# The activation of a fused recurrence and MLP rewritten: tanh(e·U(log(1 + c·e))) with one polynomial in place of two

## The chip, the core and the metric

The kernel runs on one core of one Trainium2 chip. Its engines each have an instruction queue of their own that is worked through in order: TensorE (PE, whose weight loads appear as PEld), VectorE (DVE), ScalarE (ACT), GpSimd (POOL) and SyncE (SP), which issues the DMAs here. The metric is the device time of one execution in microseconds (us); lower is better.

## The reference: what is computed

The first half is a gated recurrence over 768 steps for 4 batches of 8 heads of size 48. Its output, laid out as 3072 tokens of 384 numbers, goes through an MLP with 2048 hidden units whose activation is h·erf(softplus(h)). All of it is float32; the two weights of the MLP arrive in float64 and are rounded on the chip.

```python
f = 1.0 / (1.0 + np.exp(-f_logit))
for t in range(S):
    state = f[:, :, t, :, None] * state + np.einsum('bhd,bhe->bhde', k[:, :, t], v[:, :, t])
    y[:, :, t] = np.einsum('bhd,bhde->bhe', q[:, :, t], state)
x = y.transpose(0, 2, 1, 3).reshape(B * S, H * D)
h = x @ w_in
sp = np.maximum(h, 0.0) + np.log1p(np.exp(-np.abs(h)))
out = (h * erf(sp)) @ w_out
```

## The kernel before

**First part.** The tokens are taken in 24 chunks of 128, all heads at once (`chunk`). A chunk brings f, q and k in by transposes on PE (L318), turns f into a sigmoid F on DVE and ACT (maximum L330, Exp L333 on ACT, add L334, reciprocal L335), copies q and k out of PSUM on ACT (L338), and then climbs seven levels. At each level PE multiplies k and q into scores (L352), DVE multiplies half of q by the decays of the neighbouring half (Q, L385; the first time L375), POOL does the same to k (K, L389) and folds the decays (T, L394), and the scores are kept through a mask by DVE (At, L363), at the two last levels by copies on ACT (L371). At the end PE forms the outputs y (L403, L407), which ACT copies (xs, L411), and a new state (L419 to L438); the outputs are transposed back (L443) and copied into xT (L445).

**Second part.** Three chunks make a block of 384 tokens; there are eight blocks. For a block, `second_part` forms the 16 tiles of hidden units on PE (hps, L275, three products each), ACT copies each out of PSUM (Hg, L283, with two PSUM buffers), and after every fourth tile `activation` works on the group of four, 128 x 1536 numbers, in place. A block has four groups, called g0 to g3 here. Then three output tiles are summed on PE over all 16 tiles of hidden units (ops, L289), copied by ACT (L298) and stored.

**The activation before.** ACT takes the magnitude (Abs, L255) and Exp (L256); four quadratics follow for log1p, each a Square with a bias column on ACT (L247) and one DVE instruction that adds a constant and multiplies it into z (L250). POOL clamps h (L258), DVE adds it (L261), ACT squares the sum (L262), three more quadratics follow for erf (L247 and L250), then Tanh on ACT (L264) and the product with h on DVE (L265). The tiles e, z and x have two buffers each, so at most two groups are under way.

**What sets the order.** The second part of one block is a generator from which `chunk` draws a number of matmuls at each level of the next block's chunks: the hidden tiles during the first two chunks, the output tiles during the third. From that order and the buffers a scheduler fixes one order for each engine's queue before the program runs. An instruction that waits holds up all that stands behind it on its engine. The first block's chunks run beside the rounding of the weights, and the last block's second part runs alone at the end.

Of the kernel before, what the change touches and what calls it, by code (L numbers as in the profile page):

```python
"""HGRN2 recurrence, then x @ w_in -> h * erf(softplus(h)) -> @ w_out, all in float32.

The recurrence runs in chunks of 128 tokens.  Within a chunk, a pair (s, t), s < t, is served at the
level h = 1, 2, .., 64 at which s and t lie in neighbouring halves of a block of 2h tokens:

    prod(f[s+1..t]) = prod(f[s+1 .. end of s's half]) * prod(f[start of t's half .. t])

so q and k only ever get multiplied by products of f, which are at most 1: nothing is divided by a
decay, and nothing can overflow, whatever f is.  Going one level up multiplies half of q and half of
k by the total of the neighbouring half.  After the last level q holds the decay since the chunk's  # L10
start and k the decay to its end, which is what the state between chunks needs.

softplus(h) = max(h, 0) + log1p(exp(-|h|)), and erf on [0, inf) is tanh(z * P(z * z)).  log1p(e) / e
and P are minimax polynomials (relative error 3.0e-8 of log1p and 9.6e-8 of erf, below one float32
ulp), taken as products of quadratics (k * x + a)**2 + b.

Weights given in float64 come as their bits and are rounded to float32 here.
"""
# [17 lines left out]
# log1p(e) = e * prod((k * e + a)**2 + b) on [0, 1]  # L36
LOG1P_K = 0.518609681
LOG1P_AB = (
    (0.523462696, 0.297482162),
    (-0.0426566012, 0.876115907),  # L40
    (-0.738881803, 0.726747093),
    (-1.20404919, 0.116298437),
)
# erf(z) = tanh(z * prod((k * z * z + a)**2 + b)) for z >= 0
ERF_K = 0.072173846
ERF_AB = (
    (0.453293936, 0.100843822),
    (-0.384392197, 1.24745854),
    (-1.51376175, 0.348741268),
)  # L50
# erf(z) is 1 in float32 from here on
Z_MAX = 6.0
# exp(-x) stays finite from here on
LOGIT_MIN = -87.0

P = 128
NBUF = 3  # chunks of q, k and f on chip
LOOK = 2  # chunks that the loads run ahead
# [5 lines left out]
def kernel(  # L64
# [13 lines left out]
    wpe = 1  # 32-bit words of a weight  # L78
# [3 lines left out]
    HP = H // 2  # pairs of heads: one at partitions 0.., one at 64..  # L82
    DP = 64  # a head's rows, padded
    NCH = S // P
    CPB = 3  # chunks in a block of tokens of the second part
# [4 lines left out]
    FG = 4  # tiles of d_ff that the activation takes at once  # L90
# [11 lines left out]
    def fixed(name, shape, dtype=FP32):  # L102
        return const.tile(shape, dtype, name=name)
# [7 lines left out]
    # masks[0] is the diagonal; masks[1 + n] the pairs of level 2**n, below a block's size  # L111
# [3 lines left out]
    erf_bias = fixed("erf_bias", [P, len(ERF_AB)])  # L115
    log_bias = fixed("log_bias", [P, len(LOG1P_AB)])

# [30 lines left out]
    def load_piece(i):  # L148
        """The DMA of a piece; one in float64 lands as its words, to be rounded."""
        dst, src = pieces[i]  # L150
        if wpe == 1:
            nc.sync.dma_start(out=dst, in_=src)
            return None
        raw = gpool.tile([P, wpe * PIECE], U32, name="raw", tag="Hg")
        nc.sync.dma_start(out=raw[:].rearrange("p (k f) -> p k f", k=dst.shape[1]), in_=src)
        return raw

    def round_piece(i, raw):
        """float64 to the nearest float32: sign, exponent and 20 bits of the high word are one
        float32, the low word is what comes to it, and what is below float32's range is 0."""  # L160
# [48 lines left out]
    for i, (a, _) in enumerate(ERF_AB):  # L209
        nc.vector.memset(erf_bias[:, i : i + 1], a)  # L210
    for i, (a, _) in enumerate(LOG1P_AB):
        nc.vector.memset(log_bias[:, i : i + 1], a)
# [9 lines left out]
    for n in range(n_masks - 1):  # L222
        # s ^ t has its highest bit at n, and it is t that has it
        same = fixed(f"same{n}", [P, P], I32)
        nc.vector.tensor_scalar(
            out=bit[:], in0=col[:], scalar1=n, scalar2=1,
            op0=ALU.logical_shift_right, op1=ALU.bitwise_and,
        )
        nc.vector.tensor_scalar(
            out=same[:], in0=row[:], scalar1=n, scalar2=None, op0=ALU.logical_shift_right  # L230
        )
        nc.vector.tensor_scalar(
            out=same[:], in0=same[:], scalar1=1.0, scalar2=None, op0=ALU.is_equal
        )
        nc.vector.tensor_tensor(out=masks[:, 1 + n, :], in0=same[:], in1=bit[:], op=ALU.mult)

# [1 line left out]
    def activation(Hg):  # L238
        n = FG * TB
        h = Hg[:].rearrange("p j t -> p (j t)")  # L240
        e = work.tile([P, n], FP32, name="e", tag="e")
        z = work.tile([P, n], FP32, name="z", tag="z")
        x = work.tile([P, n], FP32, name="x", tag="x")

        def times_quads(acc, first, arg, tmp, scale, ab, bias):
            for i, (_, b_) in enumerate(ab):
                nc.scalar.activation(  # L247
                    out=tmp[:], in_=arg[:], func=AF.Square, bias=bias[:, i : i + 1], scale=scale
                )
                nc.vector.scalar_tensor_tensor(  # L250
                    out=acc[:], in0=tmp[:], scalar=b_, in1=first[:] if i == 0 else acc[:],
                    op0=ALU.add, op1=ALU.mult,
                )

        nc.scalar.activation(out=e[:], in_=h, func=AF.Abs)  # L255
        nc.scalar.activation(out=e[:], in_=e[:], func=AF.Exp, scale=-1.0)  # L256
        times_quads(z, e, e, x, LOG1P_K, LOG1P_AB, log_bias)
        nc.gpsimd.tensor_scalar(  # L258
            out=x[:], in0=h, scalar1=Z_MAX, scalar2=0.0, op0=ALU.min, op1=ALU.max
        )  # L260
        nc.vector.tensor_tensor(out=z[:], in0=z[:], in1=x[:], op=ALU.add)  # L261
        nc.scalar.activation(out=e[:], in_=z[:], func=AF.Square)  # L262
        times_quads(z, z, e, x, ERF_K, ERF_AB, erf_bias)
        nc.scalar.activation(out=z[:], in_=z[:], func=AF.Tanh)  # L264
        nc.vector.tensor_tensor(out=h, in0=h, in1=z[:], op=ALU.mult)  # L265
# [55 lines left out]
    def chunk(g, xT, fill):  # L321
# [21 lines left out]
        def scores(h):  # L343
            """k^T q of the pairs of level h (0: the diagonal) and others, to PSUM as [s, t]."""
# [104 lines left out]
    n_slots = 1 + len(levels)  # times that a chunk pumps  # L449
# [43 lines left out]
```

## Time and profile before

| | us |
|---|---|
| median of 3 runs (1463.07, 1463.49, 1740.36) | 1463.49 |
| the profiled execution, its span from first to last instruction | 1460.2 |
| difference between that median and the span | 3.3 |
| period of a block in the steady part, profile | about 160 |

In the rows below, an instruction is named by engine, line and operation, then the tile it writes and those it reads, the shape, and how many there were. "Idle before" is time in which the engine stood still just ahead of such instructions, with the engine and line whose end released it.

### The profile page before, as it was taken

To read this page: it belongs to the slowest core of one execution; us is meant where nothing else is said; L and a number is where in the kernel's file an instruction comes from. 1 tells how busy PE (TensorE), PEld (TensorE's weight loads), DVE (VectorE), ACT (ScalarE), POOL (GpSimd) and SP (SyncE) were. 2 spreads that over 40 slices of the span, in tenths; PEclk is the share of its full clock that TensorE was granted. 3 is DMA by queue.
4 is the path that set the end of the run, shared out by engine and by line. 5 is a ranking of instruction groups with operands and counts; after the bars stand their busy time and mean duration, and the time that the engine had idled before them with its cause. 6 is when DMAs were issued, how large, how long until landed. Compare 5 with 4: busy or idle time off the path is not lost.

```text
span 1460.2 us, 15916 instructions
## 1 busy us (share of the span) xinstructions
PE 1111.4 (76%) x6456; PEld 738.6 (51%) x6456; DVE 985.4 (67%) x883; ACT 686.4 (47%) x693; POOL 430.6 (29%) x401
## 2 busy tenths in 40 slices
PE   3334697689968898789959897689957998789546
PEld 2234565356535565456536565456535665455323
DVE  8896357963797357963798367963797357970682
ACT  0000047731775147731775146731775146732872
POOL 2644224232243224231252224232243124330110
PEclk9999998769966788668976898769967798669868
DMA  9330011011101011011101011011101000000000
GB/s 248 119 87 6 17 23 22 0 22 39 23 0 22 17 22 22 1 22 38 23 0 22 17 23 22 1 26 35 23 0 22 17 1 1 1 6 11 0 0 16
DMA packets 108744, 37.19 MB, mean 25 GB/s; under 512 B 100480, under 2 KB 103552, under 8 KB 108672
## 3 DMA queue, kind: packets, MB, share of 16 engines
q1 hardware_dynamic: 108672, 36.18, 11.0%
q8 instruction: 51, 0.84, 0.2%
q14 instruction: 21, 0.17, 0.0%
HBM read 31.46 MB, written 4.72 MB: 25 GB/s over the span
## 4 chain that ended last, share of the span: by engine, by line
PE 42%; DVE 30%; POOL 13%; ACT 7%; issue 6%; SPq 1%; DMA 0%; POOLq 0%; DVEq 0%; ACTq 0%
DVE z L250 13%; PE ops L289 12%; PE sc L352 8%; PE hps L275 7%; POOL K L389 6%; PE y L403 5%; PE y L407 5%; DVE F L335 4%; DVE At L363 4%; POOL x L258 3%; POOL T L394 3%; ACT x L247 3%; DVE z L261 3%; DVE Q L385 2%; PE ps_t L318 1%
## 5 line engine op out<-in xcount | busy, mean ns | idle before, releaser
L289 PE MATMUL ops<-w_out_sb,Hg 128*128 128x384 f32 x768 | 338.3, 597 | 107.9 <-DVE Hg L265 107.9
L352 PE MATMUL sc<-Q,K 48*128 48x128 f32 (+2 forms) x3456 | 246.3, 297 | 196.1 <-POOL K L389 90.3
L250 DVE SCALAR_TENSOR_TENSOR z<-x,z 128x1536 f32<-128x1536 f32 x192 | 343.6, 1807 | 47.5 <-ACT x L247 46.9
L352 PEld LDWEIGHTS sc<-Q,K 48*128 48x128 f32 (+2 forms) x3456 | 208.3, 199 | 295.4 <-POOL K L389 139.9
L389 POOL TENSOR_TENSOR K<-K,T 128x256 f32<-128x256 f32 x144 | 194.6, 1352 | 411.9 <-PE sc L352 411.3
L275 PE MATMUL hps<-xT,w_in_sb 128*128 128x384 f32 x768 | 289.8, 516 | 11.7 <-ACT Hg L283 11.0
L289 PEld LDWEIGHTS ops<-w_out_sb,Hg 128*128 128x128 f32 x768 | 171.5, 234 | 232.6 <-DVE Hg L265 91.7
L247 ACT ACTIVATE x<-e,log_bias 128x1536 f32<-128x1536 f32 x128 | 201.1, 1572 | 32.2 <-DVE z L250 29.4
L275 PEld LDWEIGHTS hps<-xT,w_in_sb 128*128 128x128 f32 x768 | 142.8, 199 | 100.2 <-ACT Hg L283 18.7
L363 DVE COPY_PREDICATED At<-masks,sc 128x1024 f32<-128x1024 uint8 x144 | 186.6, 1296 | 0.0
L247 ACT ACTIVATE x<-e,erf_bias 128x1536 f32<-128x1536 f32 x96 | 151.3, 1576 | 61.5 <-DVE z L250 58.7
L385 DVE TENSOR_TENSOR Q<-Q,T 128x256 f32<-128x256 f32 x144 | 68.4, 475 | 127.3 <-PE sc L352 126.6
L258 POOL TENSOR_SCALAR x<-Hg 128x1536 f32<-128x1536 f32 x32 | 71.6, 2237 | 255.0 <-DVE z L250 253.0
L394 POOL TENSOR_TENSOR T<-F 128x256 f32<-128x256 f32 x24 | 34.2, 1426 | 309.3 <-DVE F L335 309.3
L371 ACT COPY At<-sc 32x256 f32<-32x256 f32 (+1 forms) x72 | 31.1, 432 | 180.2 <-PE sc L352 179.8
L283 ACT COPY Hg<-hps 128x384 f32<-128x384 f32 x128 | 58.8, 471 | 102.2 <-PE hps L275 101.5
L403 PE MATMUL y<-vt,At 128*128 128x48 f32 x384 | 91.2, 339 | 0.0
L394 POOL TENSOR_TENSOR T<-T 128x128 f32<-128x128 f32 (+1 forms) x144 | 87.2, 606 | 11.3
L407 PE MATMUL y<-S_new,Q 48*128 48x48 f32 x320 | 85.0, 354 | 2.2 <-DVE Q L385 2.2
L436 DVE TENSOR_TENSOR S_new<-S_new,dS 128x192 f32<-128x192 f32 x16 | 5.7, 354 | 118.3 <-PE dS L426 118.3
L335 DVE RECIPROCAL F<-F 128x512 f32<-128x512 f32 x24 | 80.4, 3348 | 0.3
L250 DVE SCALAR_TENSOR_TENSOR z<-x,e 128x1536 f32<-128x1536 f32 x32 | 56.6, 1768 | 34.7 <-ACT x L247 34.7
(63 smaller groups left out, 948.4 us busy)
## 6 DMA issues: line engine op xcount, KB each, us to landing
raw<-in_moe_w_in_dram SPq DMA_DIRECT2D x8, 768.0 KB, 7.7
raw<-in_moe_w_out_dram SPq DMA_DIRECT2D x8, 768.0 KB, 4.2
f_nat<-in_f_logit_dram SPq DMA_DIRECT2D x24, 192.0 KB, 3.1
q_nat<-in_q_dram SPq DMA_DIRECT2D x24, 192.0 KB, 3.7
k_nat<-in_k_dram SPq DMA_DIRECT2D x24, 192.0 KB, 3.3
vt<-in_v_dram SPq DMA_DIRECT2D x24, 192.0 KB, 2.6
out_dram<-osb SPq DMA_DIRECT2D x24, 192.0 KB, 1.9
```

The lines of the kernel that those rows point to most:

```text
L247: nc.scalar.activation(out=tmp[:], in_=arg[:], func=AF.Square, bias=bias[:, i : i + 1], scale=scale)
L250: nc.vector.scalar_tensor_tensor(out=acc[:], in0=tmp[:], scalar=b_, in1=first[:] if i == 0 else acc[:], op0=ALU.add, op1=ALU.mult,)
L258: nc.gpsimd.tensor_scalar(out=x[:], in0=h, scalar1=Z_MAX, scalar2=0.0, op0=ALU.min, op1=ALU.max)
L275: nc.tensor.matmul(hps[:, 0:TB], lhsT=w_in_sb[:, kt, ft * P : (ft + 1) * P], rhs=xT[:, kt, :], start=(kt == 0), stop=(kt == n_k - 1),)
L289: nc.tensor.matmul(ops[:, 0:d_model], lhsT=groups[ft // FG][:, ft % FG, tt * P : (tt + 1) * P], rhs=w_out_sb[:, ft, :], start=(ft == 0), s ...
L335: nc.vector.reciprocal(out=F[:], in_=F[:])
L352: nc.tensor.matmul(sc[s0 : s0 + size, r, a, s0 + off : s0 + off + size], lhsT=K[rows(r), a, s0 : s0 + size], rhs=Q[rows(r), a, s0 + off : ...
L363: nc.vector.copy_predicated(out=A[:].rearrange("s r a t -> s (r a) t"), mask=masks[:, level, :].unsqueeze(1).broadcast_to((P, H, P)), data ...
L389: nc.gpsimd.tensor_tensor(out=Kv[:, :, 0, :], in0=Kv[:, :, 0, :], in1=Tv[:, :, 1:2].broadcast_to((P, n, h)), op=ALU.mult,)
L394: nc.gpsimd.tensor_tensor(out=T2[:], in0=Tv[:, :, 0], in1=Tv[:, :, 1], op=ALU.mult)
L403: nc.tensor.matmul(y_h, lhsT=A[:, r, a, :], rhs=vt[:, 2 * a + r, :], start=True, stop=(c == 0))
L407: nc.tensor.matmul(y_h, lhsT=Q[rows(r), a, :], rhs=S_old[rows(r), a, :], start=False, stop=True)
```

## The change

The activation is replaced. With e = exp(h), log(1 + c·e) comes from ACT's Ln, and one polynomial of four quadratics in it, multiplied by e, goes into Tanh:

```diff
-LOG1P_K = 0.518609681
-LOG1P_AB = (
...
-ERF_K = 0.072173846
-ERF_AB = (
...
+SERF_C = 0.885
+SERF_K = 0.30518928
+SERF_AB = (
+    (0.45453888, 0.41112006),
+    (-0.16653012, 0.6701086),
+    (-1.000969, 0.45191252),
+    (-1.3220904, 0.05253476),
 )
...
-        def times_quads(acc, first, arg, tmp, scale, ab, bias):
-            for i, (_, b_) in enumerate(ab):
-                nc.scalar.activation(
-                    out=tmp[:], in_=arg[:], func=AF.Square, bias=bias[:, i : i + 1], scale=scale
-                )
-                nc.vector.scalar_tensor_tensor(
-                    out=acc[:], in0=tmp[:], scalar=b_, in1=first[:] if i == 0 else acc[:],
-                    op0=ALU.add, op1=ALU.mult,
-                )
-
-        nc.scalar.activation(out=e[:], in_=h, func=AF.Abs)
-        nc.scalar.activation(out=e[:], in_=e[:], func=AF.Exp, scale=-1.0)
-        times_quads(z, e, e, x, LOG1P_K, LOG1P_AB, log_bias)
-        nc.gpsimd.tensor_scalar(
-            out=x[:], in0=h, scalar1=Z_MAX, scalar2=0.0, op0=ALU.min, op1=ALU.max
-        )
-        nc.vector.tensor_tensor(out=z[:], in0=z[:], in1=x[:], op=ALU.add)
-        nc.scalar.activation(out=e[:], in_=z[:], func=AF.Square)
-        times_quads(z, z, e, x, ERF_K, ERF_AB, erf_bias)
-        nc.scalar.activation(out=z[:], in_=z[:], func=AF.Tanh)
-        nc.vector.tensor_tensor(out=h, in0=h, in1=z[:], op=ALU.mult)
+        nc.scalar.activation(out=e[:], in_=h, func=AF.Exp)
+        nc.scalar.activation(out=z[:], in_=e[:], func=AF.Ln, scale=SERF_C, bias=1.0)
+        for i, (_, b) in enumerate(SERF_AB):
+            nc.scalar.activation(
+                out=x[:], in_=z[:], func=AF.Square, bias=serf_bias[:, i : i + 1], scale=SERF_K
+            )
+            nc.vector.scalar_tensor_tensor(
+                out=e[:], in0=x[:], scalar=b, in1=e[:], op0=ALU.add, op1=ALU.mult
+            )
+        nc.scalar.activation(out=e[:], in_=e[:], func=AF.Tanh)
+        nc.vector.tensor_tensor(out=h, in0=h, in1=e[:], op=ALU.mult)
```

The comments of the file go too, so all lines move up by about 20. In the changed file the activation is L235 (Exp), L236 (Ln), L238 (Square), L241 (DVE's quadratic), L244 (Tanh) and L245 (product with h); F's Exp is L313, the copies of q and k L318, the copies of hidden tiles L263, xs L391, Kn L401, scores L332, output tiles L269.

The building of the program puts a load of a function table (`ACT_TABLE_LOAD`) ahead of a function that the table at hand does not have. The program before has one such load; the changed one has 65: one at the start, 32 ahead of Ln (L236), 21 ahead of Tanh (L244), 8 ahead of the activation's Exp (L235) and 3 ahead of F's Exp (L313). The scheduler also sets the queues anew; three places follow.

ACT, second steady block, from the end of the first chunk (xs, the copy of y) to the second chunk's q and k copies. Before:

```order
L411 COPY xs<-y 128x2x4x48
L421 COPY Kn<-ps_k 128x512
L256 ACTIVATE e<-e 128x1536
L283 COPY Hg<-hps 128x384
L247 ACTIVATE x<-e,log_bias 128x1536
L333 ACTIVATE F<-F 128x512
L338 COPY Q<-ps_t 128x512
L338 COPY K<-ps_t 128x512
```

The same place in the changed program, where L235, L236 and L238 are g1's Exp, g1's Ln and g0's last Square, and L244 is g0's Tanh:

```order
L391 COPY xs<-y 128x2x4x48
L401 COPY Kn<-ps_k 128x512
L235 ACT_TABLE_LOAD
L235 ACTIVATE e<-Hg 128x1536
L238 ACTIVATE x<-z,serf_bias 128x1536
L236 ACT_TABLE_LOAD
L236 ACTIVATE z<-e 128x1536
L313 ACT_TABLE_LOAD
L313 ACTIVATE F<-F 128x512
L318 COPY Q<-ps_t 128x512
L244 ACTIVATE e<-e 128x1536
L318 COPY K<-ps_t 128x512
```

F's Exp of the second chunk stood behind three instructions after Kn, and stands now behind six and its own load; g0's Tanh stands between the copies of q and k.

PE, third chunk of the same block, from the transposes of k to the level at which the output tiles first need g3. Before:

```order
L318 MATMUL ps_t<-ident,k_nat_90 128x128 x4
L352 MATMUL sc<-Q,K 128x128 x8
L289 MATMUL ops<-w_out_sb,Hg 128x384 x8
L352 MATMUL sc<-Q,K 128x128 x24
L289 MATMUL ops<-w_out_sb,Hg 128x384 x4
L352 MATMUL sc<-Q,K 128x128 x8
```

The same place in the changed program:

```order
L298 MATMUL ps_t<-ident,k_nat_90 128x128 x4
L269 MATMUL ops<-w_out_sb,Hg 128x384 x9
L332 MATMUL sc<-Q,K 128x128 x8
L269 MATMUL ops<-w_out_sb,Hg 128x384 x7
L332 MATMUL sc<-Q,K 128x128 x8
L269 MATMUL ops<-w_out_sb,Hg 128x384 x2
L332 MATMUL sc<-Q,K 128x128 x8
L269 MATMUL ops<-w_out_sb,Hg 128x384 x2
L332 MATMUL sc<-Q,K 128x128 x16
```

In both, 24 of a block's 48 output products stand behind g3; those that need only g0 to g2 have moved from the second chunk into the third, and the first levels of scores are no longer in one run.

ACT, end of the program, from g3's first operation on. Before:

```order
L255 ACTIVATE e<-Hg 128x1536
L247 ACTIVATE x<-e,log_bias 128x1536
L264 ACTIVATE z<-z 128x1536
L256 ACTIVATE e<-e 128x1536
L247 ACTIVATE x<-e,log_bias 128x1536 x3
L262 ACTIVATE e<-z 128x1536
...
L262 ACTIVATE e<-z 128x1536
L247 ACTIVATE x<-e,erf_bias 128x1536 x3
L264 ACTIVATE z<-z 128x1536
L298 COPY osb<-ops 128x384 x3
```

The same place in the changed program:

```order
L235 ACTIVATE e<-Hg 128x1536
L238 ACTIVATE x<-z,serf_bias 128x1536
L236 ACT_TABLE_LOAD
L236 ACTIVATE z<-e 128x1536
L238 ACTIVATE x<-z,serf_bias 128x1536 x4
L244 ACT_TABLE_LOAD
L244 ACTIVATE e<-e 128x1536
L238 ACTIVATE x<-z,serf_bias 128x1536 x2
L244 ACTIVATE e<-e 128x1536
L278 COPY osb<-ops 128x384 x3
```

g2 and g3 share the stretch in both; g3's chain has become shorter, and two loads stand in it.

## Rows read from the trace of the kernel before

**Rows 1.** The page: span, then busy us (share of the span) x instructions of each engine.
```profile
span 1460.2 us, 15916 instructions
PE 1111.4 (76%) x6456; PEld 738.6 (51%) x6456; DVE 985.4 (67%) x883; ACT 686.4 (47%) x693; POOL 430.6 (29%) x401
```

**Rows 2.** Stretches: length, busy us of each engine (instructions), PE's clock, DMA.
```profile
core 0: us, PE busy (x) PEld busy (x) DVE busy (x) ACT busy (x) POOL busy (x), PEclk, DMA share, GB/s
681.00:719.00 38.00, 36.30 (x260) 23.70 (x259) 23.79 (x24) 20.91 (x26) 9.85 (x15) 0.94 0.10 21
719.00:787.00 68.00, 49.01 (x281) 31.82 (x280) 60.74 (x43) 49.87 (x45) 26.14 (x17) 0.78 0.07 12
787.00:841.00 54.00, 46.54 (x271) 30.97 (x271) 28.41 (x25) 14.99 (x18) 14.99 (x16) 0.78 0.11 26
699.30:809.50 110.20, 83.83 (x504) 54.54 (x500) 93.05 (x71) 78.27 (x72) 41.06 (x33) 0.79 0.08 15
1347.20:1439.00 91.80, 46.35 (x119) 24.67 (x117) 63.16 (x36) 70.53 (x56) 10.33 (x4) 0.78 0.00 0
```

**Rows 3.** Groups by line: busy us, mean ns of one; idle before, releaser.
```profile
L250 DVE SCALAR_TENSOR_TENSOR z<-x,z 128x1536 f32<-128x1536 f32 x192 | 343.6, 1807 | 47.5 <-ACT x L247 46.9
L250 DVE SCALAR_TENSOR_TENSOR z<-x,e 128x1536 f32<-128x1536 f32 x32 | 56.6, 1768 | 34.7 <-ACT x L247 34.7
L261 DVE TENSOR_TENSOR z<-z,x 128x1536 f32<-128x1536 f32 x32 | 59.9, 1871 | 18.9 <-POOL x L258 18.9
L265 DVE TENSOR_TENSOR Hg<-Hg,z 128x1536 f32<-128x1536 f32 x32 | 58.0, 1811 | 3.1 <-ACT z L264 3.1
L247 ACT ACTIVATE x<-e,log_bias 128x1536 f32<-128x1536 f32 x128 | 201.1, 1572 | 32.2 <-DVE z L250 29.4
L247 ACT ACTIVATE x<-e,erf_bias 128x1536 f32<-128x1536 f32 x96 | 151.3, 1576 | 61.5 <-DVE z L250 58.7
L262 ACT ACTIVATE e<-z 128x1536 f32<-128x1536 f32 x32 | 47.6, 1487 | 56.3 <-DVE z L261 56.3
L255 ACT ACTIVATE e<-Hg 128x1536 f32<-128x1536 f32 x32 | 47.5, 1485 | 1.0
L385 DVE TENSOR_TENSOR Q<-Q,T 128x256 f32<-128x256 f32 x144 | 68.4, 475 | 127.3 <-PE sc L352 126.6
L363 DVE COPY_PREDICATED At<-masks,sc 128x1024 f32<-128x1024 uint8 x144 | 186.6, 1296 | 0.0
L335 DVE RECIPROCAL F<-F 128x512 f32<-128x512 f32 x24 | 80.4, 3348 | 0.3
```

**Rows 4.** Waits: who waited for whom, us in total, times, longest us.
```profile
PE ops L289 <- DVE Hg L265: 107.9, 25, 16.4
```

**Rows 5.** Timeline of one block: start us, us, what (idle before, releaser).
```profile
558.97 0.60 PE L318 MATMUL ps_t<-ident,f_nat 128*128 128x128 f32 x4
718.86 0.60 PE L318 MATMUL ps_t<-ident,f_nat 128*128 128x128 f32 x4
699.28 1.49 ACT L255 ACTIVATE e<-Hg 128x1536 f32<-128x1536 f32 x1
720.28 0.63 ACT L333 ACTIVATE F<-F 128x512 f32<-128x512 f32 x1 [1.07 <-DVE F L330]
808.06 1.48 ACT L264 ACTIVATE z<-z 128x1536 f32<-128x1536 f32 x1 [2.43 <-DVE z L250]
```

**Rows 6.** Timeline of the end of the program, columns as above.
```profile
1347.16 1.49 ACT L255 ACTIVATE e<-Hg 128x1536 f32<-128x1536 f32 x1
1400.83 3.03 ACT L247 ACTIVATE x<-e,log_bias 128x1536 f32<-128x1536 f32 x2
1437.25 1.76 DVE L265 TENSOR_TENSOR Hg<-Hg,z 128x1536 f32<-128x1536 f32 x1 [1.55 <-ACT z L264]
1439.06 17.87 PE L289 MATMUL ops<-w_out_sb,Hg 128*128 128x384 f32 x48 [6.02 <-DVE Hg L265]
```

**Rows 7.** Timeline of ACT at the start of the program, columns as above.
```profile
0.73 1.28 ACT L338 ACT_TABLE_LOAD   x1 [0.73 <-PEq L477]
6.34 0.59 ACT L338 COPY Q<-ps_t 128x512 f32<-128x512 f32 x1 [4.33 <-PE ps_t L318]
```

More of the change, by code (lines that the diff above doesn't have):

```diff
@@ L34 @@
 PSUM = bass.MemoryType.PSUM
-LOG1P_K = 0.518609681
-LOG1P_AB = (
[L39 to L42, printed above, removed]
-)
-ERF_K = 0.072173846
-ERF_AB = (
-    (0.453293936, 0.100843822),
-    (-0.384392197, 1.24745854),
-    (-1.51376175, 0.348741268),
-)
-Z_MAX = 6.0
+SERF_C = 0.885
[5 more added lines that the diff above has]
+    (-1.3220904, 0.05253476),
+)
 LOGIT_MIN = -87.0
@@ L114 @@
     masks = fixed("masks", [P, n_masks, P], U8)
-    erf_bias = fixed("erf_bias", [P, len(ERF_AB)])
-    log_bias = fixed("log_bias", [P, len(LOG1P_AB)])
+    serf_bias = fixed("serf_bias", [P, len(SERF_AB)])
     units = [(b, c) for b in range(B) for c in range(NCH)]
@@ L208 @@
         nc.vector.memset(t[:], 0.0)
[L209 to L212, printed above, removed]
+    for i, (a, _) in enumerate(SERF_AB):
+        nc.vector.memset(serf_bias[:, i : i + 1], a)
     col = fixed("col", [P, P], I32)
@@ L243, in activation @@
         x = work.tile([P, n], FP32, name="x", tag="x")
-        def times_quads(acc, first, arg, tmp, scale, ab, bias):
-            for i, (_, b_) in enumerate(ab):
-                nc.scalar.activation(
-                    out=tmp[:], in_=arg[:], func=AF.Square, bias=bias[:, i : i + 1], scale=scale
-                )
-                nc.vector.scalar_tensor_tensor(
-                    out=acc[:], in0=tmp[:], scalar=b_, in1=first[:] if i == 0 else acc[:],
-                    op0=ALU.add, op1=ALU.mult,
-                )
-        nc.scalar.activation(out=e[:], in_=h, func=AF.Abs)
-        nc.scalar.activation(out=e[:], in_=e[:], func=AF.Exp, scale=-1.0)
-        times_quads(z, e, e, x, LOG1P_K, LOG1P_AB, log_bias)
-        nc.gpsimd.tensor_scalar(
-            out=x[:], in0=h, scalar1=Z_MAX, scalar2=0.0, op0=ALU.min, op1=ALU.max
-        )
-        nc.vector.tensor_tensor(out=z[:], in0=z[:], in1=x[:], op=ALU.add)
-        nc.scalar.activation(out=e[:], in_=z[:], func=AF.Square)
-        times_quads(z, z, e, x, ERF_K, ERF_AB, erf_bias)
-        nc.scalar.activation(out=z[:], in_=z[:], func=AF.Tanh)
-        nc.vector.tensor_tensor(out=h, in0=h, in1=z[:], op=ALU.mult)
+        nc.scalar.activation(out=e[:], in_=h, func=AF.Exp)
[9 more added lines that the diff above has]
+        nc.vector.tensor_tensor(out=h, in0=h, in1=e[:], op=ALU.mult)
     def second_part(blk, xT):
```

## The prediction

> **What bounds the kernel now.** I read the page first: over the span of 1460.2 us no engine is full, PE is busy 76% and DVE 67% [rows 1]. Such averages hide stages, so next come the stretches of one block, whose period is 718.86 − 558.97 = 159.9 us [rows 5]. Its three chunks differ [rows 2]. In the first (681 to 719) PE is busy 36.3 of 38 us: PE bounds it. In the second (719 to 787, 68 us) DVE is busy 60.7 and ACT 49.9, PE only 49.0, at a lower clock: here the activation of the block's hidden units runs, and DVE bounds. In the third (787 to 841) DVE and ACT have little to do after the first 25 us or so, but PE stands: the output tiles wait for g3's last product, and over the program such waits are 107.9 us [rows 4]. So the number to watch is the time from g0's first ACT operation (699.28) to the end of g3's Tanh (808.06 + 1.48 = 809.5): 110.2 us [rows 5]. In it ACT is busy 78.3 us and stands 31.9, DVE is busy 93.1 [rows 2]. What PE does after g3 (24 output products and the last levels) stays. At the end of the program the same chain runs alone: from 1347.2 to 1439.0, 91.8 us, ACT is busy 70.5 [rows 2], then 17.9 us of products follow [rows 6].
>
> **The change on DVE.** A group now takes four quadratics and the product with h instead of seven, an addition and that product. Removed over 32 groups: 96 of 224 quadratics, 96 x 1.80 = 173 us, and the additions, 59.9 us [rows 3]: 233 of 985 us, or 7.3 us a group and 29 us a block. The activation leaves DVE 5 x 1.8 = 9 us a group.
>
> **The change on ACT, without loads.** A group had four operations without a bias column (Abs, Exp, Square, Tanh; two are shown, 1.49 us) and seven with one (1.57) [rows 3]. Back to back they overlap: two of 1.58 took 3.03, so 0.13 is shared [rows 6], leaving 1.36 and 1.45. Before, 4 x 1.36 + 7 x 1.45 = 15.6 us a group. Ln is not in the trace; the nearest rows are the 1.49 and 1.57, and I price it as 1.45, for its operand count. At 1.36 a block would be 0.4 us shorter. Now it is 2 x 1.36 + 5 x 1.45 = 10.0. Four groups fall from 62.4 to 39.9 us: 22.5 less a block.
>
> **The loads.** 64 are added, 8 for each of the eight second parts (the order shows eight between one block's first Exp and last Tanh). The trace has one: 1.28 us [rows 7]. Behind it ACT stood 4.33 us, put down to PE, so any settling time of a load would be hidden there: the price lies between 1.28 and 1.28 + 4.33 = 5.6. I take 1.28, since the row shows that much and names another cause for the rest: 8 x 1.28 = 10.3 us a block, 82 in all. The rule that speaks against the change stands in the Trainium skill, page "ScalarE: Activation LUTs", section "What ACT_TABLE_LOAD costs": a switch of table sets is 1283 ns of load, which the row matches, and about 1380 ns of DRAIN, which no row here shows; by its 2.66 us the eight loads would be an estimated 21.3 us and eat nearly all of the 22.5.
>
> **ACT's waits in a block.** I walked ACT's new queue by hand from 699.28, with the durations above, letting each instruction start when its queue and its operands allow. ACT's work is 78.3 − 22.5 + 10.3 = 66.1. Its waits come to about 25 us now:
> - 8.4 at the copies of the last two levels' scores, in the first and second chunk: these scores need a Q product (0.48) that stands on DVE behind a quadratic (1.8), which itself needs the Square ahead of that copy. Ln and its load make this later than Abs did, so the first chunk becomes about 4 us longer than its 38.
> - 4.5 at xs, until PE has formed y.
> - 10.1 for g3 at the start of the third chunk: DVE does g2's product, the reciprocal (3.35), Q products and mask copies (1.3 each) between g3's quadratics, and with two x buffers the last Squares wait for them [rows 3].
> - 2 at copies of hidden tiles.
>
> So g3's Tanh ends 66 + 25 = 91 us after the start instead of 110.2: **19 us a block**. One price is inside: F's Exp of the second chunk, at 720.28 now [rows 5], comes out near 727, behind two loads, Exp, Square and Ln that stand ahead of it, and its own. Today DVE's backlog hides more than that in this chunk; with DVE 29 us lighter the cover is smaller, but the chunk still ends about 15 us earlier, since it needs ACT's queue and no longer DVE's. In the third chunk PE has more output products ready early (they moved there), and after g3 the same 24 remain. In alternate blocks PE has one more or one fewer level of scores to do after that, about 2 us either way. Seven blocks give 7 x 19 = 133 us.
>
> **The end of the program.** Same walk, without first part: ACT's work is 70.5 − 22.5 + 10.3 = 58.3, and it waits little, because with the next group's loads, Exp and Ln between Squares DVE keeps up. With 3.5 us of waits and the last product (1.76) that makes 63 instead of 91.8: **29 us**. PE's 17.9 us of last products follow unchanged [rows 6].
>
> **Elsewhere.** POOL loses its clamps; POOL's queue then holds only the first part. I count that as nothing: its clamps lie under DVE's backlog, and if DVE was ever held by one, the gain is a little larger. The first block and the DMAs are as before. Sum: 1460.2 − 133 − 29 = 1298 us of span; the median stands 3.3 us above the span, so **1301 us**, about 11% less.
>
> **Rivals.**
> - *A load costs about twice the row.* For it: the single load's end lies in an idle stretch, so nothing excludes it. Against: nothing in that stretch shows it. At 1.28 us more, 64 x 1.28 = 82 us of ACT time; about a fifth falls into waits, so 1301 + 66 = 1367 us. By the Trainium skill's price above it would be an estimated 5 us more.
> - *The walk is too slow, and PE becomes the bound of a block.* If DVE's and ACT's relief lets every output product be ready in time, a block needs PE's own busy time, 36.3 + 49.0 + 46.5 = 131.8 us [rows 2] instead of 159.9: 28 x 7 + 29 = 225 less, 1238 us. For it: the clock of the second and third chunk, 0.78 against 0.94 in the first, may rise if PE stands less. Against: ACT's queue, with F's Exp behind loads, delays the second chunk's start.
> - *Only the end gains.* The second and third chunks may be held by the first part's own chain of levels, so that the activation merely ends earlier into a wait. Then 1460 − 29 + 3 = 1434 us, just faster than a 2% limit, or within it if the F delay costs a few us more. Against: the first chunk climbs the same seven levels in 38 us, with 24 hidden tile products beside them, so 54 and 68 are not the levels' doing.
> - *Slower: loads at 5.6 us.* The gain of 162 us over 64 loads is 2.5 us each, so the change loses from a load of 1.28 + 2.5 = 3.8 us on. At 5.6, the row's upper bound, it is 1301 + 64 x 4.33 = 1578 us, all of it on ACT's queue ahead of Ln, Tanh and F's Exp. Against: PE's transposes, for which ACT waited, account for the whole stretch.
> - That the change does not do what it says is excluded: the order shows the 128 quadratics and the loads.
>
> **How the numbers follow.** Forecast (1250 to 1345 around 1301, by 7 us a block either way in waits): 0.50. Loads at twice the row (1345 to 1410): 0.20. PE's bound (1210 to 1250): 0.17. Only the end (1425 to 1450): 0.07. Slower: 0.06. A range from 1235 to 1390 leaves out the last two, about 0.04 of the loads' case and a part of PE's. This kernel's measurement can tell about 2% from no change, which is 1434 to 1493 us: faster 0.88, same 0.06, slower 0.06.
>
> **What would show it.** Right: 65 loads of about 1.28 us with the next ACT operation close behind; DVE near 752 us busy and ACT near 590; a block's period near 141 us; F's Exp of the second chunk some 28 us after g0's Exp, 21 now; the last Hg product 63 us after the last block's first Exp. A gap of over 1 us behind loads makes it the loads' case. Wrong would also be a Ln much longer than 1.6 us, a period near 130 with PE's waits for Hg gone, or a period still near 160 with ACT standing for PE's scores.

## The result, and the profile after

The changed kernel takes **1267.03 us** (median of four runs, 1266.77 to 1268.11) where the kernel before took 1463.49 beside it: a ratio of 0.8661 with a 95% interval of 0.8648 to 0.8674, or 196 us less. The forecast was 1301 us, and 1235 to 1390 as the range. Times and ratios here are those of fast runs: a run of the kernel before of 1740 us, one of e7 of 1468 us and one of v5_early of 5000 us are left out.

The page's first part, span and busy time of each engine, answers to [rows 1]:

```profile
span 1264.8 us, 15677 instructions
PE 1045.9 (83%) x6456; PEld 693.3 (55%) x6456; DVE 767.9 (61%) x752; ACT 574.3 (45%) x629; POOL 330.7 (26%) x369
```

DVE lost 217.5 us, ACT 112 on balance, POOL 100. PE has as many instructions as before and is 65 us less busy. The stretches of one block (an even one, whose first chunk starts a batch, as in [rows 2]), then the way from g0's Exp to g3's Tanh in that block and in the odd block ahead of it, and last the way from g0's Exp to the last product at the end of the program:

```profile
core 0: us, PE busy (x) PEld busy (x) DVE busy (x) ACT busy (x) POOL busy (x), PEclk, DMA share, GB/s
610.20:645.10 34.90, 33.92 (x251) 22.26 (x250) 22.74 (x23) 18.53 (x24) 11.27 (x14) 0.93 0.10 20
645.10:701.00 55.90, 46.09 (x289) 30.38 (x288) 39.93 (x35) 42.60 (x44) 15.15 (x15) 0.88 0.18 29
701.00:751.00 50.00, 45.11 (x274) 29.75 (x273) 24.37 (x21) 10.79 (x13) 12.94 (x15) 0.87 0.04 12
628.40:718.50 90.10, 76.50 (x527) 50.07 (x525) 68.26 (x57) 64.49 (x64) 30.24 (x30) 0.92 0.11 18
488.80:576.90 88.10, 79.46 (x510) 52.42 (x508) 63.64 (x53) 64.47 (x65) 24.76 (x27) 0.90 0.11 19
1181.40:1245.80 64.40, 48.45 (x119) 25.96 (x117) 34.61 (x20) 56.54 (x48) 0.00 (x0) 0.84 0.00 0
```

The second chunk fell from 68 to 55.9 us, and DVE no longer fills it (39.9 us). From g0's Exp to g3's Tanh it is 90.1 us where it was 110.2, and 64.4 at the end where it was 91.8. The groups that carry the change, and the four rows of loads:

```profile
L241 DVE SCALAR_TENSOR_TENSOR e<-x,e 128x1536 f32<-128x1536 f32 x128 | 228.6, 1792 | 81.7 <-ACT x L238 81.2
L238 ACT ACTIVATE x<-z,serf_bias 128x1536 f32<-128x1536 f32 x128 | 200.4, 1572 | 83.7 <-DVE e L241 83.6
L236 ACT ACTIVATE z<-e 128x1536 f32<-128x1536 f32 x32 | 47.5, 1483 | 0.4
L236 ACT ACT_TABLE_LOAD x32 | 41.1, 1283 | 0.6
L244 ACT ACT_TABLE_LOAD x21 | 26.9, 1283 | 0.4
L235 ACT ACT_TABLE_LOAD x8 | 10.3, 1283 | 0.1
L313 ACT ACT_TABLE_LOAD x3 | 3.8, 1283 | 0.1
```

Ln costs 1.48 us, the price of an operation without a bias column. What a load costs shows where one stands between two operations, here g0's Exp, the load and g0's Ln, then the copy that was queued behind them:

```profile
628.43 1.48 ACT L235 ACTIVATE e<-Hg 128x1536 f32<-128x1536 f32 x1
629.93 1.28 ACT L236 ACT_TABLE_LOAD   x1
631.22 1.48 ACT L236 ACTIVATE z<-e 128x1536 f32<-128x1536 f32 x1
632.61 0.46 ACT L263 COPY Hg<-hps 128x384 f32<-128x384 f32 x1
```

The load starts 0.02 us after Exp has ended, and Ln 0.01 after the load. With no load between them two operations overlap a little: the copy starts 1.39 us after Ln, which takes 1.48. Exp and Ln start 2.79 us apart, so a load holds ACT's queue 1.40 us longer than no load. The waits that answer to [rows 4] and to ACT's side of it:

```profile
ACT x L238 <- DVE e L241: 83.6, 47, 4.2
PE sc L332 <- POOL K L369: 90.1, 56, 10.4
PE sc L332 <- DVE Q L365: 40.7, 24, 9.7
PE ops L269 <- DVE Hg L245: 8.8, 8, 3.8
```

PE's wait for the last product of a group is down from 107.9 to 8.8 us. What it still waits for is the first part.

### The profile page after: what moved, and what is told of

The parts are those of the page before. It is cut to its first block, busy times and chain, and to the rows that moved or that the text cites. A ratio compares the mean times of both kernels' runs of the same rounds, so it can differ in the third digit from the quotient of the medians.

```text
span 1264.8 us, 15677 instructions
## 1 busy us (share of the span) xinstructions
PE 1045.9 (83%) x6456; PEld 693.3 (55%) x6456; DVE 767.9 (61%) x752; ACT 574.3 (45%) x629; POOL 330.7 (26%) x369
## 4 chain that ended last, share of the span: by engine, by line
PE 48%; DVE 21%; ACT 13%; POOL 12%; issue 5%; SPq 1%; DMA 0%; POOLq 0%; DVEq 0%; ACTq 0%
PE ops L269 15%; PE sc L332 10%; POOL K L369 8%; PE hps L255 7%; PE y L383 6%; PE y L387 5%; DVE e L241 5%; DVE F L315 5%; POOL T L374 4%; ACT x L238 3%; DVE Hg L245 2%; DVE At L343 2%; ACT z L236 2%; ACT e L235 2%; ACT L236 2%
## 5 line engine op out<-in xcount | busy, mean ns | idle before, releaser
L332 PE MATMUL sc<-Q,K 48*128 48x128 f32 (+2 forms) x3456 | 226.4, 280 | 169.7 <-POOL K L369 90.1
L332 PEld LDWEIGHTS sc<-Q,K 48*128 48x128 f32 (+2 forms) x3456 | 190.2, 184 | 271.1 <-POOL K L369 146.9
L255 PE MATMUL hps<-xT,w_in_sb 128*128 128x384 f32 x768 | 309.8, 540 | 12.0 <-ACT Hg L263 11.3
L269 PE MATMUL ops<-w_out_sb,Hg 128*128 128x384 f32 x768 | 301.9, 541 | 14.1 <-DVE Hg L245 8.8
L241 DVE SCALAR_TENSOR_TENSOR e<-x,e 128x1536 f32<-128x1536 f32 x128 | 228.6, 1792 | 81.7 <-ACT x L238 81.2
L238 ACT ACTIVATE x<-z,serf_bias 128x1536 f32<-128x1536 f32 x128 | 200.4, 1572 | 83.7 <-DVE e L241 83.6
L269 PEld LDWEIGHTS ops<-w_out_sb,Hg 128*128 128x128 f32 x768 | 153.0, 210 | 114.6 <-issue 24.5
L255 PEld LDWEIGHTS hps<-xT,w_in_sb 128*128 128x128 f32 x768 | 148.2, 209 | 100.7 <-issue 19.5
L365 DVE TENSOR_TENSOR Q<-Q,T 128x256 f32<-128x256 f32 x144 | 80.1, 556 | 148.8 <-PE sc L332 148.7
L263 ACT COPY Hg<-hps 128x384 f32<-128x384 f32 x128 | 58.7, 471 | 110.1 <-PE hps L255 110.0
L374 POOL TENSOR_TENSOR T<-T 128x128 f32<-128x128 f32 (+1 forms) x144 | 72.1, 501 | 11.3
L383 PEld LDWEIGHTS y<-vt,At 128*128 128x128 f32 x384 | 66.2, 220 | 13.8 <-ACT At L351 0.4
L387 PEld LDWEIGHTS y<-S_new,Q 48*128 48x128 f32 x320 | 57.8, 225 | 11.7 <-DVE Q L365 1.4
```

Source lines behind the costliest of these rows:

```text
L238: nc.scalar.activation(out=x[:], in_=z[:], func=AF.Square, bias=serf_bias[:, i : i + 1], scale=SERF_K)
L241: nc.vector.scalar_tensor_tensor(out=e[:], in0=x[:], scalar=b, in1=e[:], op0=ALU.add, op1=ALU.mult)
L255: nc.tensor.matmul(hps[:, 0:TB], lhsT=w_in_sb[:, kt, ft * P : (ft + 1) * P], rhs=xT[:, kt, :], start=(kt == 0), stop=(kt == n_k - 1),)
L269: nc.tensor.matmul(ops[:, 0:d_model], lhsT=groups[ft // FG][:, ft % FG, tt * P : (tt + 1) * P], rhs=w_out_sb[:, ft, :], start=(ft == 0), s ...
L332: nc.tensor.matmul(sc[s0 : s0 + size, r, a, s0 + off : s0 + off + size], lhsT=K[rows(r), a, s0 : s0 + size], rhs=Q[rows(r), a, s0 + off : ...
L365: nc.vector.tensor_tensor(out=Qv[:, :, 1, :], in0=Qv[:, :, 1, :], in1=Tv[:, :, 0:1].broadcast_to((P, n, h)), op=ALU.mult,)
```

## The experiments

All times are medians of runs on a chip beside runs of the kernel before, which lay between 1461 and 1463 us there.

**e1, no loads.** One function is replaced:

```diff
-        nc.scalar.activation(out=z[:], in_=e[:], func=AF.Ln, scale=SERF_C, bias=1.0)
+        nc.scalar.activation(out=z[:], in_=e[:], func=AF.Tanh, scale=SERF_C, bias=1.0)
```

> Leaves out the logarithm: Ln is replaced by Tanh with the same scale and bias, so that 64 of the 65 table loads go and the count of ACT's operations stays. Theory, the loads stand on the path: 64 x 1.283 = 82 us leave ACT, and as in the prediction about four fifths are felt, so 1267 - 66 = 1201 us, with a block near 132. Rival, the loads lie in ACT's waits (it is busy 45% of the span): 1255 to 1267 us. PE's own busy time, 125 to 128 us of a block of 140.5, allows at most 7 x 14 = 98 us in the blocks.

Measured: 1225.8 us, ratio 0.8383 (0.8358 to 0.8409), 41 us under the changed kernel. Half of the 82 us of loads is felt, neither four fifths nor nothing. The queues were set anew without the loads, so a part of the difference may be the order.

**e4, twice the loads.** Behind each Ln:

```diff
+        nc.scalar.activation(out=t1[:], in_=z[:, 0:1], func=AF.Exp)
+        nc.scalar.activation(out=z[:, 0:1], in_=t1[:], func=AF.Ln, scale=1.0, bias=0.0)
```

> The changed kernel with an Exp and a Ln of one column behind each Ln, which bring two more table loads a group: 64 loads and 64 tiny operations more, about 64 x (1.28 + 0.2) = 95 us of ACT. Theory, loads are on the path at their price in the trace: 0.8 x 95 = 76, 1343 us, and e1 mirrors it. Rival, loads lie in ACT's waits: under 1290 us. If a load had a hidden cost of about its own length, it would be over 1400 us.

Measured: 1330.2 us, ratio 0.9087 (0.9054 to 0.9121), 63 us over the changed kernel for 64 loads and 64 tiny operations. ACT's busy time rose from 574.3 to 666.9, by the first part of its page:

```profile
PE 1057.8 (80%) x6456; PEld 696.7 (52%) x6456; DVE 766.7 (58%) x752; ACT 666.9 (50%) x757; POOL 319.9 (24%) x369
```

Two of its groups of loads, those ahead of Ln (L237 here) and of the added Ln (L239):

```profile
L237 ACT ACT_TABLE_LOAD x32 | 41.1, 1283 | 0.6
L239 ACT ACT_TABLE_LOAD x32 | 41.1, 1283 | 0.6
```

So 63 of 93 us are felt, 0.68, and each load is 1.283 us again. With e1 this brackets the share at a half to two thirds of ACT's added time; the forecast took 0.8 where it priced the loads' rival.

**e2, DVE's work of before, in the chain.** Ahead of Tanh:

```diff
+        for _, b in SERF_AB[:3]:
+            nc.vector.scalar_tensor_tensor(
+                out=e[:], in0=x[:], scalar=b, in1=e[:], op0=ALU.add, op1=ALU.mult
+            )
+        nc.vector.tensor_tensor(out=e[:], in0=e[:], in1=x[:], op=ALU.add)
```

> The changed kernel with four more DVE instructions of 128 x 1536 in each group's chain (three quadratics more and an addition, so another function is computed): DVE's work as before the change, ACT's and POOL's as after. 32 x 7.3 = 233 us of DVE return. Theory, DVE bounded the second chunk before, so relief of DVE is the larger part of the gain: 7 x 13 + 20, about 1375 us. Rival, the gain came from ACT's shorter work, and DVE has room: under 1305 us.

Measured: 1465.0 us, ratio 1.0014 (0.9998 to 1.003). The whole gain is gone, although ACT, with its loads, is 107 us less busy than before the change. Its block answers to [rows 2], first, second and third chunk:

```profile
684.50:718.70 34.20, 33.23 (x250) 21.81 (x250) 22.56 (x23) 18.49 (x24) 11.06 (x14) 0.95 0.10 20
718.70:788.00 69.30, 51.60 (x287) 33.75 (x286) 57.98 (x43) 42.22 (x41) 17.06 (x15) 0.77 0.07 12
788.00:847.00 59.00, 47.76 (x277) 32.55 (x277) 32.39 (x28) 12.03 (x16) 11.91 (x15) 0.76 0.10 24
```

The second chunk is back at 69 us with DVE busy 58 of them. Still, e2 lengthens each group's chain at one place, behind its last Square, where the kernel before had the quadratics spread between Squares.

**e5, DVE's work of before, beside the chain.** The same four instructions, on z in place of e, which nobody reads afterwards:

```diff
+        for _, b in SERF_AB[:3]:
+            nc.vector.scalar_tensor_tensor(
+                out=z[:], in0=x[:], scalar=b, in1=z[:], op0=ALU.add, op1=ALU.mult
+            )
+        nc.vector.tensor_tensor(out=z[:], in0=z[:], in1=x[:], op=ALU.add)
```

> As e2, the same four DVE instructions of 128 x 1536 for each group, but beside the chain: they work on z after the last Square has read it, and Tanh does not wait for them (their result is dropped). It tells DVE's occupancy from the length of a group's chain. Theory, DVE's queue bounded the second chunk, so occupancy alone costs most of e2's 198 us: over 1400 us. Rival, the added length of the chain (7.3 us a group, the last group's above all) made e2 slow: under 1330 us.

Measured: 1410.5 us, ratio 0.9652 (0.9616 to 0.9687). Beside the chain the same work still costs 143 us; in the chain it costs 55 more (e2). The 143 us are not occupation alone: on DVE's queue mostly two of the four instructions stand ahead of the group's product with h, which comes that much later.

**e7, DVE's work in the chain, no loads.** e2 with Ln replaced by Tanh as in e1:

> e2 (DVE's work of before the change in the chain) with Ln replaced by Tanh, which leaves out the logarithm and the 64 loads: ACT has 10.0 in place of 15.6 us a group and no load, DVE and the chain's DVE part are as before the change. e2 was at the time of before, 1465 us. Theory, DVE's occupied queue bounds by itself, and ACT's shorter work brings nothing without it: 1430 to 1465 us. Rival, the loads ate what ACT's shorter work would have brought in e2: 64 x 1.28 = 82 us, 1380 us or less.

Measured: 1444.8 us, ratio 0.9902 (0.9869 to 0.9935). With DVE's work of before in the chain, the shorter ACT work is worth about 14 us by that ratio without loads, and nothing with them.

**e3, ACT's work of before, in the chain.** Abs ahead of Exp, and four operations behind Ln:

```diff
-        nc.scalar.activation(out=e[:], in_=h, func=AF.Exp)
+        nc.scalar.activation(out=e[:], in_=h, func=AF.Abs)
+        nc.scalar.activation(out=e[:], in_=e[:], func=AF.Exp)
...
+        nc.scalar.activation(out=z[:], in_=z[:], func=AF.Square)
+        for i in range(3):
+            nc.scalar.activation(
+                out=z[:], in_=z[:], func=AF.Square, bias=serf_bias[:, i : i + 1], scale=SERF_K
+            )
```

> The changed kernel with Abs ahead of Exp and four more Squares behind Ln in each group (another function is computed): ACT's operations as before the change and Ln and the loads on top, DVE's as after. 5 operations or 7.1 us a group, 28 a block, 226 in all. Theory, after the change ACT's queue sets the length from g0's Exp to g3's Tanh: about 20 us a block and 25 at the end are felt, 1267 + 165 = 1432 us. Rival, ACT's waits of 25 us a block take most of it in: under 1330 us.

Measured: 1415.8 us, ratio 0.9684 (0.9665 to 0.9702), 149 us over the changed kernel for 229 us more of ACT's busy time, near the theory's 165. What ACT's queue now holds up is seen in PE's waits for the copies of hidden tiles, 54.2 us for hidden tiles and 47.2 for output tiles, where the changed kernel shows 11.3 and 5.1:

```profile
PE hps L261 <- ACT Hg L269: 54.2, 31, 9.2
PE ops L275 <- ACT Hg L269: 47.2, 7, 10.6
```

**e6, ACT's work of before, beside the chain.** Five operations on z behind the last Square, into a tile that nobody reads:

```diff
+        s = work.tile([P, n], FP32, name="s", tag="s", bufs=1)
+        nc.scalar.activation(out=s[:], in_=z[:], func=AF.Abs)
+        nc.scalar.activation(out=s[:], in_=z[:], func=AF.Square)
+        for i in range(3):
+            nc.scalar.activation(
+                out=s[:], in_=z[:], func=AF.Square, bias=serf_bias[:, i : i + 1], scale=SERF_K
+            )
```

> As e3, five more ACT operations of 128 x 1536 a group, but beside the chain: Abs and four Squares of z into a tile that nobody reads, behind the group's last Square. The scheduler gives it 61 table loads in place of 65. Theory, ACT's occupied queue is what e3's 149 us came from, since Tanh, Hg copies and the first part's copies stand behind it: 1380 to 1420 us. Rival, the chain's length (7.1 us a group) did it: under 1330 us.

Measured: 1439.8 us, ratio 0.9841 (0.9818 to 0.9864). Beside the chain the same work costs more, 173 us (its trace has 65 loads, not 61). So the operations need not be in the chain to be felt. But e6 does not tell ACT's occupied queue from a longer way to Tanh: on that queue all five stand ahead of the group's Tanh, which comes later too. Why it costs 24 us more than e3 stays open; PE's waits for the copies of hidden tiles are 95.8 us here.

**e8, POOL's clamp back.** Into a tile that nobody reads:

```diff
+        s = work.tile([P, n], FP32, name="s", tag="s", bufs=1)
+        nc.gpsimd.tensor_scalar(out=s[:], in0=z[:], scalar1=6.0, scalar2=0.0, op0=ALU.min, op1=ALU.max)
```

> The changed kernel with POOL's clamp back, 128 x 1536 once a group into a tile that nobody reads (32 x 2.24 = 72 us of POOL). The prediction counted the clamp at nothing: 1265 to 1275 us. Rival, the first part's products and folds on POOL (K, T), on which PE waits 90 us after the change, stand behind it: 72 us on the path at most, and over 1290 us if a third is.

Measured: 1275.3 us, ratio 0.8726 (0.8707 to 0.8746): 8 us for the clamp. The clamps took 48.1 us here, not the 72 expected:

```profile
L245 POOL TENSOR_SCALAR s<-z 128x1536 f32<-128x1536 f32 x32 | 48.1, 1503 | 210.0 <-ACT z L236 209.6
```

This is small, though not nothing. What the clamp cost inside the chain, where DVE's addition waited 18.9 us for it [rows 3], no run shows.

**Four versions that might be faster.** *v2_x4* gives each Square an x tile of its own:

```diff
-        x = work.tile([P, n], FP32, name="x", tag="x")
...
         for i, (_, b) in enumerate(SERF_AB):
+            x = work.tile([P, n], FP32, name="x", tag="x", bufs=4)
             nc.scalar.activation(
...
```

> The changed kernel with a tile x of its own for each Square, from four buffers, in place of one x a group from two. In the trace after the change ACT's Squares wait 83.6 us for DVE's quadratics, since the four Squares of a group write one tile. Theory, a third to a half of these waits lie on the path: 1225 to 1245 us. Rival, DVE's queue is behind them and the wait only moves to Tanh: 1260 to 1270 us.

Measured: 1291.2 us, ratio 0.882 (0.8788 to 0.8852), slower than the changed kernel by 24 us. The Squares no longer wait; they run in fours or in twos, and what stands behind them on ACT is late. From its timeline of ACT in the second chunk, with waits in brackets:

```profile
662.37 5.98 ACT L238 ACTIVATE x<-z,serf_bias 128x1536 f32<-128x1536 f32 x4
668.25 0.85 ACT L263 COPY Hg<-hps 128x384 f32<-128x384 f32 x2
674.30 0.48 ACT L263 COPY Hg<-hps 128x384 f32<-128x384 f32 x1 [5.21 <-PE hps L255]
675.06 1.48 ACT L244 ACTIVATE e<-e 128x1536 f32<-128x1536 f32 x1 [0.28 <-DVE e L241]
```

And its waits that took the place of the 83.6 us:

```profile
ACT e L244 <- DVE e L241: 53.0, 16, 6.0
PE hps L255 <- ACT Hg L263: 33.1, 17, 9.2
```

Two copies wait out 6 us of Squares, PE's hidden tiles wait for them (33.1 us in all, 11.3 before), and Tanh now waits for DVE (53.0 us, 18.5 before). With one x tile, DVE's pace had left gaps in which the copies went.

The stretch shows how copies come late, but not where the time was lost: its block is an even one, and from chunk start to chunk start it takes 140.4 us (first row below; 140.8 in the changed kernel). The four odd blocks take 151.5, 140.0, 146.2 and 151.3 us, where the changed kernel's take 142.7, 139.2, 139.1 and 139.9. In them g2's Exp comes 46 to 52 us after g0's, 32 to 39 in the changed kernel. The last three of the four have the same order on every engine, and their lengths go with PE's granted clock (columns as in the stretches above):

```profile
620.50:760.90 140.40, 125.16 (x811) 82.00 (x810) 85.12 (x77) 71.03 (x79) 38.67 (x44) 0.89 0.10 21
480.50:620.50 140.00, 123.66 (x807) 81.05 (x806) 84.99 (x76) 70.65 (x78) 39.13 (x44) 0.93 0.12 23
760.90:907.10 146.20, 129.63 (x808) 84.91 (x807) 85.08 (x76) 70.64 (x78) 39.10 (x44) 0.89 0.11 22
1047.30:1198.60 151.30, 135.57 (x806) 89.19 (x805) 85.55 (x77) 70.65 (x78) 39.12 (x44) 0.84 0.01 5
```

How the 24 us divide between the late copies and PE's slower passes is not shown.

*v4_pair_ln* takes Ln once for two groups, which halves the loads:

```diff
...
+        z = work.tile([P, 2 * n], FP32, name="z", tag="z", bufs=1)
+        nc.scalar.activation(out=z[:], in_=pairs[-1][0][:], func=AF.Ln, scale=SERF_C, bias=1.0)
...
```

> The changed kernel with Ln taken once for two groups (128 x 3072) and each Square with an x tile of its own from two buffers: 33 table loads in place of 65. e1 gave 41 us for 64 loads, so 32 fewer give about 20: 1245 us, if the later start of a pair's first quadratics is hidden by DVE's other work. Rival, waiting for the pair's second group lengthens the way to the last Tanh by some 5 us a block: 1280 us or more.

Measured: 1268.9 us, ratio 0.8675 (0.8648 to 0.8702), the same as the changed kernel. It also has an x tile for each Square, from two buffers, so it is not told here whether pairing or those tiles took back what 32 loads fewer should give.

*v5_early* draws two thirds of the hidden tiles in the first chunk:

```diff
-    per_chunk = [n_hidden // 2, n_hidden - n_hidden // 2, n_project]
+    per_chunk = [n_hidden * 2 // 3, n_hidden - n_hidden * 2 // 3, n_project]
```

> The changed kernel with two thirds of a block's hidden tiles drawn in the first chunk in place of half (per_chunk 32, 16, 48), so that g1 and g2 start earlier and the first output tiles can go into the second chunk. PE is busy 125 to 128 of a block's 140.5 us after the change, so at most 7 x 13 = 91 us can be had. Theory, ACT's queue from g0's Exp to g3's Tanh sets a block, and it starts earlier against the first part: 1225 to 1250 us. Rival, the first chunk grows by what the others lose: 1260 to 1280 us.

Measured: 1289.5 us, ratio 0.8821 (0.8806 to 0.8836), even above the rival's 1280. Where the 22 us went stays open: there is no profile of a run of that length.

*v7_prio* puts the start of a chunk ahead of the activation where both are ready:

```diff
+        with tc.high_priority():
             ps = transposed(nat["f"][g % NBUF])
...
```

> The changed kernel with a higher priority in the scheduler for the beginning of a chunk (transposes of f, q and k, F, copies of q and k). On ACT the copy of k now stands ahead of g0's Tanh in the second chunk, and F's Exp with both copies ahead of g2's Tanh at the start of the third; the eight loads a block stay. After the change the copy of k in the second chunk came 1.4 us after that Tanh, and F's Exp of the third 2.8 us after a load and Tanh. Theory, the start of a chunk is on the path and the chunk that follows moves with it: 2 to 4 us a block, 1240 to 1255 us. Rival, the activation's chain is delayed by as much: 1262 to 1272 us.

Measured: 1268.2 us, ratio 0.8665 (0.8638 to 0.8693), the same. In the later even blocks F's Exp of the third chunk comes 1.7 us sooner after g0's Exp than in the changed kernel (68.6 for 70.3), but g2's Tanh ends 1.2 later and g3's 0.2; the later odd blocks show the same times in both. None of the versions that compute the reference's function beats the changed kernel.

## Why the prediction was right, and where it was off

**The bound and the mechanism.** DVE bounded the second chunk, as read from [rows 2]: with its work back in the chain the gain is gone (e2), and beside the chain it still takes back 143 of the 196 us (e5). That ACT's queue is on the path after the change is shown by e3 and e6: of 229 and 223 us of added work, 149 and 173 are felt. That it alone sets the time is not shown. Of the 219 us that e5 adds to DVE, 143 are felt, the same share as in e3, and no run makes DVE lighter still. The two sides do not add up. ACT's side alone (with POOL's clamps gone) brings 0 us when DVE's work of before stands in the chain, 52 when it stands beside it (e2, e5), and 14 in the chain without loads (e7); DVE's alone, under an ACT that is even busier than before, 47 (e3); both together 196. So while the work of one side stays, half or more of the relief of the other falls into waits, although neither queue is full: in e2's second chunk DVE is busy 58 of 69 us.

**The loads.** The price was the one row's 1.28 us, and that is what all 64 take, with 0.01 to 0.02 us around them. The rival that a load costs about twice that is out; the DRAIN that the Trainium skill's page "ScalarE: Activation LUTs" counts beside a load ("What ACT_TABLE_LOAD costs") is not seen between these operations. The slower rival falls with it. The walk took 1.28 us for a load and an overlap for every operation; as a load overlaps with neither neighbour, that is 0.12 a load or 1 us a block too little. That a load is felt only by a half to two thirds was not needed for the sum, which walked ACT's queue, but the loads' rival was priced with 0.8.

**A block: the term that was off.** The forecast was 19 us a block, the measured mean is 23.6: from the first chunk with hidden tiles (186.1 us in both kernels) to the hidden tiles of the end (1336.3 before, 1170.8 after) the seven blocks took 1150.2 and take 984.7 us, 165.4 less where 133 was forecast. That is 32 of the 34 us that the forecast was too high. I had walked one even block and put its 159.9 and 110.2 us down for all seven. It is the shortest of the seven: from chunk start to chunk start they take 160.6 to 166.0 us before the change, 164.3 in the mean (the "about 160" above is too low). In the three even blocks 21.2 us were gained, close to the 19 forecast, in the four odd ones 25.5, which makes 26 of the 32 us. In an odd block the first chunk continues a batch, PE forms y in twice as many products, and the way from g0's first operation to g3's Tanh was longer before the change:

```profile
533.20:648.60 115.40, 92.35 (x520) 60.52 (x516) 92.04 (x71) 78.60 (x72) 39.38 (x32) 0.76 0.08 14
```

That row is the kernel before, in an odd block. It fell to 88.1, by 27.3; the even block's 110.2 to 90.1, by 20.1. A small part is seen at xs in the first chunk, where ACT waits for y in odd blocks only: 3.61 us before (first line), 1.64 after, with g1's Exp and its load ahead of xs. Where the rest of the difference went is not shown.

```profile
552.64 0.48 ACT L411 COPY xs<-y 128x384 f32<-128x384 f32 x1 [3.61 <-PE y L407]
502.15 1.28 ACT L235 ACT_TABLE_LOAD   x1
503.44 1.48 ACT L235 ACTIVATE e<-Hg 128x1536 f32<-128x1536 f32 x1
506.56 0.48 ACT L391 COPY xs<-y 128x384 f32<-128x384 f32 x1 [1.64 <-PE y L387]
```

**ACT's waits.** The total was forecast at 25 us a block, and 90.1 − 64.5 = 25.6 were measured, but that is luck: two of its terms did not come, one was left out, and they cancelled. The 8.4 us at the copies of scores, with a first chunk 4 us longer, did not come: the scheduler put the first quadratic behind the Q product that those scores need, the copies waited 0.4 us, and the first chunk became shorter (34.9 for 37.5 us from transposes to transposes in the even block). In their place stands a term that I had left out: the four Squares of a group share one x tile, and not two, so each waits for DVE's quadratic on the one before; outside g3's end that is 8.5 us in this block. The 2 at copies of hidden tiles did not come. The 4.5 at xs was 5.3, and the 10.1 for g3 at the start of the third chunk, walked with two x tiles, was 10.5 with one, at these four places:

```profile
705.98 1.58 ACT L238 ACTIVATE x<-z,serf_bias 128x1536 f32<-128x1536 f32 x1 [4.21 <-DVE e L241]
709.85 1.58 ACT L238 ACTIVATE x<-z,serf_bias 128x1536 f32<-128x1536 f32 x1 [2.29 <-DVE e L241]
713.25 1.58 ACT L238 ACTIVATE x<-z,serf_bias 128x1536 f32<-128x1536 f32 x1 [1.83 <-DVE e L241]
716.99 1.48 ACT L244 ACTIVATE e<-e 128x1536 f32<-128x1536 f32 x1 [2.17 <-DVE e L241]
```

F's Exp of the second chunk came 22.8 us after g0's Exp, where 28 was forecast and 21 was before; the difference is the 4 us that the first chunk did not grow by, and a little more. (After Kn it stands behind five instructions and its own load, not six.)

**The end of the program.** Forecast 29 us less, and 63 from g0's Exp to the end of the last product with h; measured 64.4, which is 27.4 less than before. PE's products behind it, put down as unchanged, end 15.8 us later and not 17.9:

```profile
1237.45 24.12 PE L269 MATMUL ops<-w_out_sb,Hg 128*128 128x384 f32 x64 [3.77 <-DVE Hg L245]
1244.01 1.76 DVE L245 TENSOR_TENSOR Hg<-Hg,e 128x1536 f32<-128x1536 f32 x1 [1.55 <-ACT e L244]
```

From the start of the hidden tiles to the end of the span it is 94.0 us where it was 123.9, or 29.9 less. The term holds in size, and a part of that is luck.

**DVE and ACT in all.** DVE was forecast near 752 us and is busy 767.9, ACT near 590 and is 574.3. DVE's Q products are 11.7 us of the former (L365, 80.1 us, for 68.4 [rows 3]); Ln at 1.48 in place of 1.57 is 3 us of the latter, and the rest was not followed.

**The other rivals.** PE's bound gave 1238 us from PE's busy time of before; the result lies between it and the forecast. PE is busy 33.9 + 46.1 + 45.1 = 125.1 of the block's 140.8 us, so it is not yet the bound. Only the end gains: out, since seven blocks gave 165 us.

## What to carry to other kernels

Where two queues feed one chain, price a change to both by walking the queue that will be the longer one, instruction by instruction, with what stands ahead of each wait; engine totals would have given neither 0, 47 nor 196 us. Walk every kind of block once before multiplying by their number: here two kinds alternated, and the one that was not walked gave 4 us more a block. A buffer that makes an engine wait can be what keeps its queue open for others, so look at what stands behind the waiting instruction before taking the wait away.

## What the runs showed of the hardware that was not expected

PE's granted clock in the second and third chunk rose from 0.78 and 0.78 [rows 2] to 0.88 and 0.87, without any change to PE's instructions. (Such a figure is a mean over time at PE's two levels, 2.4 GHz as 1 and 1.2 GHz as 0.5.) PE stood less between its instructions, and the 768 passes for the output tiles (L289 before, L269 after) went from 597 to 541 ns each, while those for the hidden tiles (L275, L255) went from 516 to 540. Over the seven blocks PE's busy time fell from 952.9 to 888.7 us. How much of the gain this is was not measured apart, but blocks of one kernel with the same order on every engine bear on it. In v2_x4's last three odd blocks, shown above, PE's busy time differs by 11.9 us and the length by 11.3, with DVE, ACT and POOL alike. In the kernel before, two such odd blocks differ by 4.9 us in PE's busy time and only by 0.5 in length:

```profile
515.30:681.30 166.00, 140.82 (x807) 92.80 (x806) 111.86 (x92) 85.50 (x86) 49.70 (x48) 0.79 0.09 19
841.90:1007.40 165.50, 135.97 (x807) 90.02 (x806) 112.24 (x92) 85.37 (x86) 49.21 (x48) 0.82 0.09 19
```

So in the odd blocks of the kernel before, PE's slower passes fell into waits, which fits DVE as the bound. Whether the changed kernel's blocks would follow the clock is not shown: from the third on they all have 0.89. Means over a whole span tell little: e1 has 0.928, e2 0.828, the kernel before 0.832 and the changed one 0.889, while the runs of v4_pair_ln took 1270.4 us at 0.852 and 1265.1 to 1271.8 at 0.896 to 0.898.
